# Row maxima turned by a product with the identity on TensorE, and their one transfer issued by ScalarE on its own queue

## The chip, the cores and the metric

The kernel runs on 1 core of one Trainium2 chip. The metric is the device time of one execution in microseconds (us). Engines are named as in the profile: PE is TensorE's matmul, PEld its weight load, DVE is VectorE, ACT is ScalarE, POOL is GpSimd, SP is SyncE, whose queue issues DMA transfers.

## The reference, cut to what matters

Two attentions over the same `x` (2048 tokens, 640 wide, 32 heads of 20) are mixed by a gate per token. A is causal attention inside segments of 512 tokens with a linear memory carried from segment to segment. B is sliding-window attention with a window of 256.

```python
x = A_x
g = sigmoid((x * gate_w).sum(-1, keepdims=True))
# A, per segment s of 512 tokens
p = softmax(qs @ ks.T * Dh**-0.5 + causal_mask)
o = gate * (phi(qs) @ M) / (phi(qs) @ z + 1e-6) + (1 - gate) * (p @ vs)
M, z = M + phi(ks).T @ vs, z + phi(ks).sum()
# B, window of 256
p = softmax(where(mask, q @ k.T * Dh**-0.5, -1e9));  o = p @ v
out = g * (a @ A_wo) + (1 - g) * (b @ B_wo)
```

Each softmax needs, for every query, the maximum of its row of scores before the exponent is taken. The change is about how these maxima reach the second score product.

## The kernel before, in words

**Stages and tiles.** The work is cut into 16 tiles `T`, four head groups (two of A, two of B) times four segments. For each tile, `gemm` (L429) projects q and k as three products of split float32 parts, `v_mm` (L543) projects v, and the parts of q and k are written to DRAM (`qk_store`, L477) and read back as stacks (`stack_read`, L604) with the head's dimension on partitions. Each tile then gives four units `u` of four heads, 64 units in all. A q stack `qst` has 123 used rows for each head: 120 hold the split parts of q, and the last three (from row `6 * DH`) hold the row maximum as three bfloat16 parts, so that the second score product subtracts the maximum by itself.

**A unit.** `max_mm` (L622) makes the scores once, queries on partitions, 16 products per unit. `max_red` (L633) on DVE adds the mask and takes the maximum over the keys, one column of the tile `mx` for each head and block of 128 queries: 16 columns on 128 partitions. These maxima have to be split into three bfloat16 parts and turned so that queries lie on the free axis, since they become rows of `qst`. Then `st_mm` (L687) makes the scores again with keys on partitions and the maxima subtracted, `st_exp` (L694) on ACT takes the exponent, `select` (L700, L703) on POOL clears what the mask forbids, `av_mm` (L717) multiplies by v, and `o_turn` (L796) to `o_store` (L836) divide and store. `o_load` (L849 to L860) reads the heads' outputs back for the output projection, again `gemm`, with results added by `y_out` (L868, L871).

**The maxima's way before the change.** `max_res` (L643, POOL) subtracts the upper bfloat16 half from the 16 maxima. `max_high` (L646, ACT) copies the upper halves of maximum and remainder into `mrs`, and `max_low` (L650, POOL) puts the third part there. `max_turn` (L654, DVE) transposes `mrs` in blocks of 32 by 32 into `mt`. `max_store` (L660, SP, two transfers) writes `mt` to DRAM as `dmx`, 64 bytes at a time, which finishes the turn. `max_rows` (L664, SP) waits until both have landed and reads three rows of `dmx` into `qst`. All transfers of the kernel are issued by SP, in one order.

**What sets the order.** `Plan` holds every step with a due time, the engine, an assumed duration and what it reads and writes. `Plan.order` (L94) walks through them like a list scheduler: of the steps whose inputs are there, the one that can start first comes next, and the earlier due time decides ties. Each engine gets its steps in that order, and runs them in that order on the chip whatever happens there. A transfer is modelled as landing a fixed time plus its share of 16 rings after its issue. So a step that is made shorter, or is moved to another engine, changes what the plan puts beside it, and the order of the whole program. Due times of the steps above are in units: the first products at `u - MT`, the maxima's way at `u - MS`, the second products from `u + 0.04`.

The two PE steps read and write PSUM banks, of which there are eight, dealt out by the plan by kind: `mx` three, `st` two, `misc` two, `pj` three to seven.

Of the kernel before, what the change touches and what calls it, by code (L numbers as in the profile page):

```python
# [20 lines left out]
DH = 20  # L21
S = 2048
L = 512
# [14 lines left out]
NPX, NMI, NOB = 7, 2, 2  # L38
# [16 lines left out]
class Plan:  # L55
# [13 lines left out]
    RINGS = 16  # L69

    def add(self, t, eng, dur, fn, *a, new=(), mod=(), put=(), get=(), size=0, pace=None, cols=0, ldw=(0.107, 0.2),
            bank=None, lazy=0.0, rings=16, packet=2048, port=False):
        if size:
            size = (size / packet / rings * (0.011 + packet / 21e3), rings)
        self.items.append((t, len(self.items), eng, dur, fn, a, new, mod, put, get, size, pace, cols, ldw, bank, lazy, port))

    TICK = 10.24 / 3
# [16 lines left out]
    def order(self):  # L94
# [85 lines left out]
        while len(out) < n:  # L180
            best = None
            for e, c in cand.items():
                cold = e == "pe" and self.cold(free[e])
                for i in c:
                    at = free[e]
                    if e == "pe":
                        at += max(0.0, items[i][13][0] - tail)
                    z = max(at, ready[i]) + (items[i][15] if tail > 0.06 else 0.0)
                    if items[i][16] and e in ("dve", "pool"):
                        z = max(z, port)  # L190
                    if items[i][14]:
                        k, most, _ = items[i][14]
                        if not avail or held.get(k, 0) >= most:
                            continue
                        z = max(z, min(avail.values()))
                    if e == "dve" and "|" in items[i][2]:
                        z += DP
                    z = (z, cold and items[i][12] < 900, i)
                    if best is None or z < best[0]:
                        best = (z, e)  # L200
            (start, _, i), e = best
            start -= DP if e == "dve" and "|" in items[i][2] else items[i][15] if e == "pe" and tail > 0.06 else 0.0
            if items[i][14]:
# [36 lines left out]
            if j is not None:  # L240
                ready[j] = max(ready[j], start)
                miss[j] -= 1
                if not miss[j]:
                    offer(j)
            for j in succ[i]:
                to = items[j][2]
                lag = ((0.0 if e == "pe" else XS) if to == e and not size else self.TO_PE if to == "pe" else
                       0.0 if size else self.FROM_PE if e == "pe" else self.OTHER)
                ready[j] = max(ready[j], done + lag)
                miss[j] -= 1  # L250
                if not miss[j]:
                    offer(j)
# [19 lines left out]
def attention(ctx, tc, const, dram, xt, wqk, wv, wo, beta, ident, o_dram, out):  # L272
# [17 lines left out]
            nc.tensor.matmul(p[:, 0:256], ones[:, 0:128], ones, start=True, stop=True)  # L290

    idf = const.tile([128, 128], F32, name="idf")

    mask_a = const.tile([128, 512], BF16, name="mask_a")
    mask_b = const.tile([128, 384], BF16, name="mask_b")
# [15 lines left out]
    def c_load():  # L311
        nc.sync.dma_start(idf, ident)
        nc.sync.dma_start(bet, bass.AP(tensor=beta.tensor, offset=beta.offset, ap=[[8, 4], [0, 32], [1, 8]]))

    def c_exp():
        nc.scalar.activation(gh[:, 0], bet, AF.Exp, scale=-1.0)

# [8 lines left out]
    vau = [stack.tile([128, n, VROW], F32, name=f"vau{i}") for i, n in enumerate((4, 6, 6))]  # L326


    mrs = [stack.tile([128, 64], BF16, name=f"mrs{i}") for i in range(2)]
# [8 lines left out]

    def init_m():
        nc.gpsimd.memset(pks, 0.0)  # L340
        for t in mrs:
            nc.gpsimd.memset(t, 0.0)

    def init_v(i):
        t = vau[i]
# [13 lines left out]
    NT = NSG * NSEG  # L359
    NU = 4 * NT  # L360
    PE, ACT, DVE, POOL, SP = "pe", "act", "dve", "pool", "sp"
    DI, DJ, SI = 0.48, 0.65, 0.53

    def unit(u):
        T, g = divmod(u, 4)
# [259 lines left out]
    def max_red(u, p, b, r):  # L625
        T, g, isb, s = unit(u)
        w = max_keys(u, b)[1]
        mk = mask_b[:, 384 - w:] if isb else mask_a[:, 512 - w:]
        if p == 0 and b == 0 and r == 0:
            B["M", u] = work.tile([128, 32], F32, name="mx", tag="mx")  # L630
        x = B["mx", u, p, b, r][:, :w]
        j = 4 * (2 * p + r) + b
        nc.vector.tensor_tensor_reduce(out=x, in0=x, in1=mk, scale=1.0,  # L633
                                       scalar=BIG, op0=ALU.add, op1=ALU.max, accum_out=B["M", u][:, j:j + 1])

    def high(x):

        return x.bitcast(BF16).rearrange("p (j c) -> p j c", c=2)[:, :, 1]

    def max_res(u):  # L640

        x = B["M", u]
        nc.gpsimd.tensor_tensor(out=x[:, 16:32], in0=x[:, 0:16], in1=high(x[:, 0:16]), op=ALU.subtract)  # L643

    def max_high(u):
        nc.scalar.activation(mrs[u % 2][:, 0:32], high(B["M", u]), AF.Copy)  # L646

    def max_low(u):
        x = B["M", u][:, 16:32]
        nc.gpsimd.tensor_tensor(out=mrs[u % 2][:, 32:48], in0=x, in1=high(x), op=ALU.subtract)  # L650

    def max_turn(u):
        t = B["mt", u] = work.tile([128, 64], BF16, name="mt", tag="mt")
        nc.vector.transpose(t, mrs[u % 2])  # L654

    def max_store(u, i):
        if i == 0:
            B["dmx", u] = dram.tile([4, 4, L], BF16, name="dmx", tag="dmx", bufs=3)
        d = B["dmx", u]
        nc.sync.dma_start(bass.AP(tensor=d.tensor, offset=d.offset + 8 * L * i, ap=[[32, 4], [128, 32], [1, 32]]),  # L660
                          B["mt", u][:, 32 * i:32 * i + 32])

    def max_rows(u):
        nc.sync.dma_start(qst[u % NQ][6 * DH:6 * DH + 3], B["dmx", u][0:3])  # L664

# [253 lines left out]
    add(-13, POOL, 2.0, c_mask, put=["mk"])  # L919
    add(-25, PE, 0.107 * WARM, c_warm, bank=("warm", 1, "warm"), cols=256 * WARM)  # L920
    add(-16.5, SP, 1.1, c_load, put=["cl"], size=2 ** 16)
    add(-3, ACT, 0.25, c_exp, get=["cl"], put=["ce"])
    add(-3, DVE, 1.2, c_fac, get=["cl", "ce"], put=["cf"])

# [62 lines left out]
    for u in range(NU):  # L987
# [12 lines left out]
                    new=[("M", 2, ("M", u))] if i == 0 and r == 0 else [],  # L1000
                    put=[("M", u)] if i or r else [])
        t = u - MS
        add(t, POOL, 0.2, max_res, u, mod=[("M", u)], port=True)
        add(t + .001, ACT, 0.24, max_high, u, get=[("M", u), "im"], new=[("mr", 2, ("mr", u))])
        add(t + .002, POOL, 0.2, max_low, u, get=[("M", u)], put=[("mr", u)], port=True)
        add(t + .01, DVE, 0.165, max_turn, u, get=[("mr", u)], new=[("mt", 2, ("mt", u))])
        for i in range(2):
            add(t + .03 + .001 * i, SP, DJ, max_store, u, i, get=[("mt", u)], size=8192, packet=64,
                new=[] if i else [("dmx", 3, ("dmx", u))], put=[("dmx", u)] if i else [])
        add(t + .04, SP, DJ, max_rows, u, get=[("dmx", u)], put=[("qr", u)], size=12288, packet=1024, rings=3)  # L1010
        for i in range(6):
            b, p = divmod(i, 2)
            t = u + 0.04 + i / 6
# [103 lines left out]
```

## Time and profile before

| | |
|---|---|
| time, median of 3 runs | 1183.43 us (1181.92 to 1185.99) |
| the profiled execution | 1172.0 us, span 1170.3 us |
| mean granted TensorE clock | 0.982 |
| busy: PE, POOL, DVE, ACT | 1095.5, 815.5, 780.8, 703.7 us |
| DMA | 221.35 MB, all but the code on one queue, 74.5% of 16 engines' span |

Busy time of an engine leaves out its waits and the issuing of transfers. A wait is put down to what ended last before the waiting instruction could start. In the view of waits each row has who waited, for whom, us in total, how often, and the longest. In the chain of waits each row has the start in us from the span's begin, the length, and what the program's end depended on then. In the view by windows each row has the stretch, busy time of each engine, the granted clock, the DMA engines' share and GB/s. In the groups each row ends with busy us, mean ns of one, and the idle time of the engine before them.

### The profile page before, as it was taken

To read this page: it belongs to the slowest core of one execution; us is meant where nothing else is said; L and a number is where in the kernel's file an instruction comes from. 1 tells how busy PE (TensorE), PEld (TensorE's weight loads), DVE (VectorE), ACT (ScalarE), POOL (GpSimd) and SP (SyncE) were. 2 spreads that over 40 slices of the span, in tenths; PEclk is the share of its full clock that TensorE was granted. 3 is DMA by queue.
4 is the path that set the end of the run, shared out by engine and by line. 5 is a ranking of instruction groups with operands and counts; after the bars stand their busy time and mean duration, and the time that the engine had idled before them with its cause. 6 is when DMAs were issued, how large, how long until landed. Compare 5 with 4: busy or idle time off the path is not lost.

```text
span 1170.3 us, 25017 instructions
## 1 busy us (share of the span) xinstructions
PE 1095.5 (94%) x8322; PEld 717.0 (61%) x8322; DVE 780.8 (67%) x2641; ACT 703.7 (60%) x1495; POOL 815.5 (70%) x1063
## 2 busy tenths in 40 slices
PE   9788999997999999999898999998997999999996
PEld 7564666664655666556565566655664666766664
DVE  3475877765778667786586866777664776577711
ACT  6246575675557765575664767665664595655651
POOL 9345484796667786678774778667795686866874
PEclk9999999998999999999899999999998999999999
DMA  6877588878988589877788867888577885887523
GB/s 211 163 188 182 162 207 198 202 185 160 240 203 208 149 217 233 217 196 207 147 217 176 234 163 186 206 223 204 148 176 203 219 215 140 205 205 211 161 91 108
DMA packets 228081, 221.35 MB, mean 189 GB/s; under 512 B 80240, under 2 KB 189168, under 8 KB 227952
## 3 DMA queue, kind: packets, MB, share of 16 engines
q1 hardware_dynamic: 227952, 219.75, 74.5%
q8 instruction: 66, 1.08, 0.4%
q14 instruction: 63, 0.52, 0.2%
HBM read 154.73 MB, written 64.95 MB: 188 GB/s over the span
## 4 chain that ended last, share of the span: by engine, by line
PE 58%; DMA 23%; POOL 6%; DVE 5%; SPq 4%; issue 3%; ACT 2%; POOLq 0%; ACTq 0%; DVEq 0%
PE bank L429 22%; PE bank L687 10%; PE bank L717 9%; PE bank L622 8%; PE bank L543 8%; DMA qst<-dmx 3%; DMA qst<-dqk 3%; DMA dmx<-mt 3%; DMA xst<-wv 3%; DVE bank L633 3%; DMA kst<-dqk 2%; DMA wst<-wqk 2%; DMA xst<-o_dram 2%; DMA xst<-xt 1%; SPq L604 1%
## 5 line engine op out<-in xcount | busy, mean ns | idle before, releaser
L694 ACT ACTIVATE P<-bank 128x512 f32<-128x512 f32 (+2 forms) x768 | 372.0, 563 | 94.1 <-PE bank L687 80.0
L429 PE MATMUL bank<-xhl,w 128*128 128x512 f32 x1200 | 366.4, 431 | 1.8 <-POOL xhl L394 0.6
L633 DVE CUSTOM_DVE_ANT_0 bank<-bank,mask_b 128x384 f32<-128x384 f32 (+2 forms) x512 | 259.3, 552 | 53.0 <-PE bank L622 51.9
L633 DVE CUSTOM_DVE_ANT_0 bank<-bank,mask_a 128x128 f32<-128x128 f32 (+3 forms) x512 | 237.9, 511 | 71.6 <-PE bank L622 70.3
L622 PE MATMUL bank<-kst,qst 120*128 120x384 bf16 (+3 forms) x1024 | 253.1, 312 | 21.1 <-DVE mx L633 9.8
L687 PE MATMUL bank<-qst,kst 123*128 123x384 bf16 (+2 forms) x1216 | 233.0, 291 | 36.7 <-DMA qst<-dmx 28.3
L429 PEld LDWEIGHTS bank<-xhl,w 128*128 128x128 f32 x1200 | 219.2, 193 | 46.5 <-issue 1.7
L394 POOL TENSOR_TENSOR w<-wst,w 128x640 fp32r<-128x640 f32 x119 | 185.3, 1558 | 70.2 <-ACT w L378 63.0
L700 POOL TENSOR_SCALAR_AFFINE_SELECT P<-P 128x512 f32<-128x512 f32 x256 | 160.7, 636 | 79.5 <-ACT P L694 76.3
L543 PE MATMUL bank<-wv,xhl 128*128 128x320 f32 (+1 forms) x960 | 189.5, 335 | 1.3 <-POOL wv L394 0.7
L429 PE MATMUL bank<-ohl,w 128*128 128x512 f32 x600 | 178.9, 425 | 5.9 <-POOL w L394 2.6
L687 PEld LDWEIGHTS <-kst 123*128 123x128 bf16 x1216 | 92.0, 99 | 138.4 <-issue 74.0
L717 PE MATMUL bank<-P,vau 128*32 128x384 f32 (+3 forms) x2432 | 160.8, 408 | 1.8 <-POOL P L703 0.9
L543 PEld LDWEIGHTS bank<-wv,xhl 128*128 128x128 f32 x960 | 152.5, 192 | 12.3 <-DVE mx L633 2.7
L622 PEld LDWEIGHTS <-qst 120*128 120x128 bf16 x1024 | 81.5, 98 | 123.8 <-issue 86.6
L633 DVE DVE_READ_ACCUMULATOR2_ANT mx<- 128x1 f32 x1024 | 142.8, 140 | 0.0
L446 POOL TENSOR_TENSOR hl<-res,hl 128x512 bf16<-128x512 f32 x104 | 121.2, 1167 | 30.3 <-ACT hl L378 28.0
L796 DVE STREAM_TRANSPOSE ot<-bank 128x512 f32<-128x512 f32 x88 | 62.7, 714 | 99.3 <-PE bank L717 94.6
L429 PEld LDWEIGHTS bank<-ohl,w 128*128 128x128 f32 x600 | 108.8, 191 | 31.4 <-POOL ohl L394 5.0
L378 ACT ACTIVATE w<-wst 128x640 fp32r<-128x640 f32 x121 | 89.9, 744 | 54.5 <-PE bank L429 17.7
L717 PEld LDWEIGHTS bank<-P,vau 128*32 128x32 f32 x2432 | 68.8, 110 | 83.8 <-issue 66.3
L394 POOL TENSOR_TENSOR wv<-xst,wv 128x322 fp32r<-128x322 f32 x79 | 68.3, 877 | 34.6 <-ACT wv L378 32.5
(73 smaller groups left out, 910.8 us busy)
## 6 DMA issues: line engine op xcount, KB each, us to landing
wst<-wqk SPq DMA_DIRECT2D x80, 320.0 KB
o_dram<-ot SPq DMA_DIRECT2D x64, 256.0 KB
qst<-dqk SPq DMA_DIRECT2D x64, 240.0 KB
kst<-dqk SPq DMA_DIRECT2D x64, 240.0 KB
wst<-wo SPq DMA_DIRECT2D x41, 320.0 KB
xst<-wv SPq DMA_DIRECT2D x80, 161.0 KB
dqk<-hl SPq DMA_DIRECT2D x32, 384.0 KB
qst<-dqk SPq DMA_DIRECT2D x64, 160.0 KB
```

The lines of the kernel that those rows point to most:

```text
L378: nc.scalar.activation(dst, src, AF.Copy)
L394: EN[e].tensor_tensor(out=t[:, 1], in0=B.pop(src), in1=f(t[:, 0]), op=ALU.subtract)
L429: nc.tensor.matmul(p, w[:, a, col:col + 128], x[:, b], start=(c == 0 and i == 0), stop=(c == NC - 1 and i == 2))
L446: EN[e].tensor_tensor(out=t[:, 2], in0=B["res", k], in1=t[:, 1], op=ALU.subtract)
L543: nc.tensor.matmul(p[:, :n], x[:, a, 128 * b:128 * b + 128], w[:, bb, :n], start=(c == 0 and i == 0), stop=(c == NC - 1 and i == 2))
L622: nc.tensor.matmul(pt[:, :n], qst[u % NQ][0:6 * DH, h, 128 * b:128 * b + 128], kst[u % NK][0:6 * DH, h, c0:c0 + n], start=True, stop=True)
L633: nc.vector.tensor_tensor_reduce(out=x, in0=x, in1=mk, scale=1.0, scalar=BIG, op0=ALU.add, op1=ALU.max, accum_out=B["M", u][:, j:j + 1])
L687: nc.tensor.matmul(pt[:, c:c + 128 * n], kst[u % NK][0:6 * DH + 3, h, c0:c0 + 128], q[0:6 * DH + 3, h, 128 * q0:128 * (q0 + n)], start=Tru ...
L694: nc.scalar.activation(B["P", u, b][:, 2 * p + r, c0:c1], B["st", u, b, p, r][:, c0:c1], AF.Exp, scale=SCALE)
L700: nc.gpsimd.affine_select(out=v, in_=v, pattern=[[0, 4], [1, 128]], compare_op=ALU.is_ge, fill=0.0, base=0, channel_multiplier=-1)
L717: nc.tensor.matmul(o[32 * j:32 * j + 32, 128 * q0:128 * (q0 + n)], v[:, VA * h:VA * h + 32], t[:, j, c:c + 128 * n], start=(b == 0 and i = ...
L796: nc.vector.transpose(B["ot", u][:, i].rearrange("p b e -> p (b e)"), B["o" if i == 0 else "num", u])
```

## The change

The upper halves of the maxima need no copy: they are read in place by `high`, a view of every second bfloat16 in `mx`. So `mx` gets 48 columns, and two subtractions on POOL, one after the other, leave maximum, first remainder and second remainder there. `max_turn` is now a product on PE: the 48 upper halves are its weights, a bfloat16 identity of 128 by 128 (`idb`, made once by ACT from `idf`) streams through, and 48 rows of 128 queries come out in a PSUM bank of the kind `misc`. `max_out` on ACT copies them to `mt` in SBUF. `max_rows` is one transfer of 48 rows of 256 bytes from `mt` straight to the three rows of `qst`, issued by ACT. `mrs`, `dmx`, the two stores to DRAM, the copy and the transpose are gone. In the plan, a transfer marked `side` doesn't queue on the 16 modelled rings: it lands 1.2 us and twice its own time after its issue, and the usual fixed part later.

```diff
-            size = (size / packet / rings * (0.011 + packet / 21e3), rings)
+            size = (size / packet / rings * (0.011 + packet / 21e3), rings, side)
...
-                took, rings = size
-                done = 0.0
-                for k in range(rings):
+                took, rings, side = size
+                done = start + dur + 1.2 + 2 * took if side else 0.0
+                for k in range(0 if side else rings):
...
-    def max_res(u):
+    def max_res(u, i):
         x = B["M", u]
-        nc.gpsimd.tensor_tensor(out=x[:, 16:32], in0=x[:, 0:16], in1=high(x[:, 0:16]), op=ALU.subtract)
+        a = x[:, 16 * i:16 * i + 16]
+        nc.gpsimd.tensor_tensor(out=x[:, 16 * i + 16:16 * i + 32], in0=a, in1=high(a), op=ALU.subtract)
-    def max_high(u):
-        nc.scalar.activation(mrs[u % 2][:, 0:32], high(B["M", u]), AF.Copy)
-    def max_low(u):
-        x = B["M", u][:, 16:32]
-        nc.gpsimd.tensor_tensor(out=mrs[u % 2][:, 32:48], in0=x, in1=high(x), op=ALU.subtract)
     def max_turn(u):
-        t = B["mt", u] = work.tile([128, 64], BF16, name="mt", tag="mt")
-        nc.vector.transpose(t, mrs[u % 2])
-    def max_store(u, i):
...
+        nc.tensor.matmul(psum(("mp", u))[0:48, 0:128], high(B["M", u]), idb, start=True, stop=True)
+    def max_out(u, e):
+        t = B["mt", u] = work.tile([48, 128], BF16, name="mt", tag="mt")
+        copy(e, t, B["mp", u][0:48, 0:128])
     def max_rows(u):
-        nc.sync.dma_start(qst[u % NQ][6 * DH:6 * DH + 3], B["dmx", u][0:3])
+        nc.scalar.dma_start(qst[u % NQ][6 * DH:6 * DH + 3].rearrange("p h (b t) -> p (h b) t", b=4), B["mt", u])
...
-        add(t, POOL, 0.2, max_res, u, mod=[("M", u)], port=True)
-        add(t + .001, ACT, 0.24, max_high, u, get=[("M", u), "im"], new=[("mr", 2, ("mr", u))])
-        add(t + .002, POOL, 0.2, max_low, u, get=[("M", u)], put=[("mr", u)], port=True)
-        add(t + .01, DVE, 0.165, max_turn, u, get=[("mr", u)], new=[("mt", 2, ("mt", u))])
         for i in range(2):
-            add(t + .03 + .001 * i, SP, DJ, max_store, u, i, get=[("mt", u)], size=8192, packet=64,
-                new=[] if i else [("dmx", 3, ("dmx", u))], put=[("dmx", u)] if i else [])
-        add(t + .04, SP, DJ, max_rows, u, get=[("dmx", u)], put=[("qr", u)], size=12288, packet=1024, rings=3)
+            add(t + .001 * i, POOL, 0.2, max_res, u, i, mod=[("M", u)], port=True)
+        add(t + .01, PE, 0.06, max_turn, u, bank=("misc", NMI, ("mp", u)), get=[("M", u), "id"], cols=102, ldw=(0.02, 0.05))
+        add(t + .02, ACT, 0.22, max_out, u, "act", get=[("mp", u)], new=[("mt", 2, ("mt", u))])
+        add(t + .03, ACT, DQ, max_rows, u, get=[("mt", u)], put=[("qr", u)], size=12288, packet=256, rings=3, side=True)
```

The order moves everywhere. Three places at the last unit, 63, show how. On PE before the change, ahead of the first second score product of unit 63 (L687 with `qst3` and `kst3`) stand output projections (L429) and unit 62's product with v (L717, tile `vau2`):

```order
L429 MATMUL bank_15422<-ohl_15312,w_15135 128x512 x3
L429 MATMUL bank_15422<-ohl_15318,w_15135 128x512 x3
L717 MATMUL bank_15455<-P_15370,vau2_97 32x384 x4
L717 MATMUL bank_15455<-P_15370,vau2_97 32x128 x4
L717 MATMUL bank_15455<-P_15396,vau2_97 32x384 x4
L717 MATMUL bank_15455<-P_15396,vau2_97 32x128 x4
L717 MATMUL bank_15455<-P_15426,vau2_97 32x256 x8
L687 LDWEIGHTS kst3_90
L687 MATMUL bank_15489<-qst3_94,kst3_90 128x384
```

On PE in the change, the turn of unit 63's maxima (L650) stands in the same row of work, and the second score products (now L680) follow after one projection (now L431, three products) and unit 62's product with v (now L710, 24 instructions, which are 48 products in the trace):

```order
L431 MATMUL bank_15277<-ohl_15211,w_15101 128x512 x3
L650 LDWEIGHTS mx_15068
L650 MATMUL bank_15308<-idb_83,mx_15068 48x128
L431 MATMUL bank_15277<-ohl_15259,w_15101 128x512 x3
L710 MATMUL bank_15330<-P_15218,vau2_98 32x384 x4
L710 MATMUL bank_15330<-P_15218,vau2_98 32x128 x4
L710 MATMUL bank_15330<-P_15253,vau2_98 32x384 x4
L710 MATMUL bank_15330<-P_15253,vau2_98 32x128 x4
L710 MATMUL bank_15330<-P_15286,vau2_98 32x256 x8
L680 LDWEIGHTS kst3_91
L680 MATMUL bank_15357<-qst3_95,kst3_91 128x384
```

So PE itself now has a step of the maxima's way, in the middle of its other work, and what it does between the turn and the scores is given by this row. On SP before the change, unit 63's two stores (L660) and its read (L664) stand among loads of heads' outputs (L857, L860) and a store of them (L836):

```order
L660 DMA dmx_15355<-mt_15353 4x32x32
L860 DMA xst_15358<-o_dram1_63 120x1x512
L857 DMA xst_15358<-o_dram1_63 8x512
L857 DMA xst_15372<-o_dram1_63 12x512
L860 DMA xst_15372<-o_dram1_63 100x1x512
L857 DMA xst_15372<-o_dram1_63 16x512
L660 DMA dmx_15355<-mt_15353 4x32x32
L857 DMA xst_15401<-o_dram1_63 4x512
L860 DMA xst_15401<-o_dram1_63 120x1x512
L857 DMA xst_15401<-o_dram1_63 4x512
L836 DMA o_dram1_63<-ot_15364 128x512
L664 DMA qst3_94<-dmx_15355 3x2048
```

On SP in the change (L853, L850 and L829 are the lines that were L860, L857 and L836; L867 stores results, L388 loads weights) nothing of the maxima is left:

```order
L853 DMA xst_15238<-o_dram1_63 100x1x512
L850 DMA xst_15238<-o_dram1_63 16x512
L867 DMA out<-ys_14390 128x512
L388 DMA wst_15262<-wo 128x640
L829 DMA o_dram1_63<-ot_15220 128x512
L850 DMA xst_15315<-o_dram1_63 4x512
L853 DMA xst_15315<-o_dram1_63 120x1x512
L850 DMA xst_15315<-o_dram1_63 4x512
```

The transfer stands on ACT instead, behind the exponents of unit 62 (L687 now, tile `P`) and right behind the copy of the turned maxima (L380, tile `mt`):

```order
L687 ACTIVATE P_15286<-bank_15274 128x512
L687 ACTIVATE P_15286<-bank_15288 128x512
L687 ACTIVATE P_15286<-bank_15294 128x512
L380 ACTIVATE mt_15311<-bank_15308 48x128
L657 DMA qst3_95<-mt_15311 3x16x128
L861 ACTIVATE ys_15324<-bank_15277 128x512
L380 ACTIVATE w_15326<-wst_15140 128x640
```

What moved there: the way from turned maxima to `qst` left DVE and SP, and now leads over PE and ACT, each of which has other steps of its order ahead of it. At other units up to eight other steps of ACT stand between the copy and the transfer; at 53 of the 64 it is one or none.

More of the change, by code (lines that the diff above doesn't have):

```diff
@@ L71, in add @@
     def add(self, t, eng, dur, fn, *a, new=(), mod=(), put=(), get=(), size=0, pace=None, cols=0, ldw=(0.107, 0.2),
-            bank=None, lazy=0.0, rings=16, packet=2048, port=False):
+            bank=None, lazy=0.0, rings=16, packet=2048, port=False, side=False):
         if size:
-            size = (size / packet / rings * (0.011 + packet / 21e3), rings)
+            size = (size / packet / rings * (0.011 + packet / 21e3), rings, side)
         self.items.append((t, len(self.items), eng, dur, fn, a, new, mod, put, get, size, pace, cols, ldw, bank, lazy, port))
@@ L292, in attention @@
     idf = const.tile([128, 128], F32, name="idf")
+    idb = const.tile([128, 128], BF16, name="idb")
     mask_a = const.tile([128, 512], BF16, name="mask_a")
@@ L313, in c_load, with c_id @@
         nc.sync.dma_start(bet, bass.AP(tensor=beta.tensor, offset=beta.offset, ap=[[8, 4], [0, 32], [1, 8]]))
+    def c_id():
+        nc.scalar.activation(idb, idf, AF.Copy)
     def c_exp():
@@ L326, in attention @@
     vau = [stack.tile([128, n, VROW], F32, name=f"vau{i}") for i, n in enumerate((4, 6, 6))]
-    mrs = [stack.tile([128, 64], BF16, name=f"mrs{i}") for i in range(2)]
     pks = stack.tile([128, L], F32, name="pks")
@@ L340, in init_m @@
         nc.gpsimd.memset(pks, 0.0)
-        for t in mrs:
-            nc.gpsimd.memset(t, 0.0)
     def init_v(i):
@@ L361, in attention @@
     PE, ACT, DVE, POOL, SP = "pe", "act", "dve", "pool", "sp"
-    DI, DJ, SI = 0.48, 0.65, 0.53
+    DI, DJ, SI, DQ = 0.48, 0.65, 0.53, 0.4
     def unit(u):
@@ L629, in max_red @@
         if p == 0 and b == 0 and r == 0:
-            B["M", u] = work.tile([128, 32], F32, name="mx", tag="mx")
+            B["M", u] = work.tile([128, 48], F32, name="mx", tag="mx")
         x = B["mx", u, p, b, r][:, :w]
@@ L921, in attention @@
     add(-16.5, SP, 1.1, c_load, put=["cl"], size=2 ** 16)
+    add(-3, ACT, 0.25, c_id, get=["cl"], put=["id"])
     add(-3, ACT, 0.25, c_exp, get=["cl"], put=["ce"])
```

5 lines of the change are left out of this document (removed).

## The prediction

> **What bounds the kernel now.** First the page's busy times, then who made PE wait, then the stretches in which it waited.
>
> ```profile
> span 1170.3 us, 25017 instructions
> PE 1095.5 (94%) x8322; PEld 717.0 (61%) x8322; DVE 780.8 (67%) x2641; ACT 703.7 (60%) x1495; POOL 815.5 (70%) x1063
> PE bank L687 <- DMA qst<-dmx: 28.3, 10, 7.7
> PE bank L622 <- DVE mx L633: 9.8, 10, 7.5
> PE bank L687 <- DVE mx L633: 4.9, 5, 2.7
> PE bank L622 <- DMA kst<-dqk: 3.9, 2, 2.9
> PE bank L687 <- ACT P L694: 2.0, 4, 0.8
> ```
>
> PE is busy for 1095.5 of 1170.3 us, so 74.8 us of idle time are all that a change of waits can win, but for the clock. The largest single part, 28.3 us in 10 waits, is the second score product waiting for the read of the maxima from DRAM, the very transfer that the change replaces. The next, DVE's maxima, make 14.7 us in two rows. Where do they lie?
>
> ```profile
> 260.00:345.00 85.00, 75.64 (x565) 48.62 (x563) 56.03 (x194) 46.13 (x108) 55.16 (x73) 0.94 0.84 198
> 560.00:600.00 40.00, 34.77 (x281) 23.21 (x280) 22.09 (x73) 24.91 (x55) 26.35 (x39) 0.91 0.80 167
> 860.00:900.00 40.00, 32.29 (x230) 21.41 (x220) 18.57 (x66) 20.80 (x45) 24.75 (x33) 0.91 0.85 197
> 1127.00:1171.00 44.00, 34.01 (x171) 23.44 (x169) 5.12 (x8) 11.11 (x19) 21.31 (x19) 0.99 0.31 93
> ```
>
> In the first three stretches PE is idle for 9.4, 5.2 and 7.7 us, and its granted clock is 0.94, 0.91 and 0.91: the waits also bring half clock. Put as time at half clock, 0.09 missing in 40 us is 7.2 us, twice, and 0.06 in 85 us is 10.2 us, together 24.6. The chain of waits shows what happens there, and at the last unit and two others:
>
> ```profile
> 571.45 8.80 DMA qst<-dmx
> 872.64 9.42 DMA dmx<-mt
> 882.13 7.37 DMA qst<-dmx
> 1059.58 2.44 DMA qst<-dmx
> 1114.12 4.04 DMA dmx<-mt
> 1118.23 2.83 DMA qst<-dmx
> ```
>
> Each unit's maxima go through two transfers, one after the other: 16.8 us in the middle of the kernel, 6.9 at its end, where the fourth stretch shows the DMA engines at 0.31. A 12 KB read takes 2.44 to 2.83 us with little ahead of it, and 7.37 to 8.80 in the queue that everything shares.
>
> **The change part by part.** The sum is made against the profiled execution, 1172.0 us, which is 11.4 below the median of the three runs shown; I carry the difference over to that median.
>
> *The waits for `qst<-dmx`.* They go with the transfer: -28.3. What is late next at those places is counted below as new waits.
>
> *Half clock.* Of the 24.6 us, part was idle anyway, and the rest did half the work. At most 12 us come back, at least nothing; I take -4, since the waits themselves fill most of those windows.
>
> *The tail.* Unit 63's way from first store to scores is 6.9 us at 1114, and becomes shorter by 2 to 3 us for each transfer saved. Behind it PE is idle for 10.0 of the last 44 us, but other work fills part of what is won: -4, between 0 and -6.5.
>
> *64 products on PE.* The nearest rows are products of the chain, weight loads included:
>
> ```profile
> 595.22 0.45 PE bank L687 x4
> 603.37 0.43 PE bank L622 x2
> 591.90 1.40 PE bank L429 x6
> 586.82 1.33 PE bank L543 x9
> 601.08 2.29 PE bank L717 x32
> 588.85 2.73 PE bank L717 x48
> 598.91 0.39 PE bank L755 x32
> L622 PEld LDWEIGHTS <-qst x1024: 95/98/152, 41.7 to 1105.8; 120*128 120x128 bf16 x171
> ```
>
> A product of 48 weights and 128 columns lies between 0.39/32 = 0.012 us (32 columns) and 0.45/4 = 0.113 (256 on average). It is nearest to the latter: 0.1, so 64 x 0.1 = +6.4, between 0.8 and 13.8 (0.43/2 each, at the upper end).
>
> *A new wait on PE, for POOL.* `max_turn` stands in PE's order behind both subtractions, and behind it wait all products that follow. What waited for them until now:
>
> ```profile
> DVE mt L654 <- POOL mrs L650: 37.8, 19, 6.9
> ACT mrs L646 <- POOL mx L643: 29.3, 21, 4.3
> PEld bank L717 <- POOL P L700: 3.4, 8, 0.9
> PEld bank L717 <- POOL P L703: 2.8, 5, 1.0
> ```
>
> DVE lost 37.8 us so. PE as the fullest engine tends to come late: for POOL's selects, which stand in front of 64 groups of products with v, its loads wait 6.2 us in 13 waits, 0.5 us each. Between 0 and 37.8, nearer to PE's own rows: +8.
>
> *A new wait on PE, for the new transfer.* This decides most. The plan now leaves less PE work between turn and scores. At unit 63 it is one projection and one product with v: 1.40/2 + 2.73 = 3.4 us. Counting the order's steps the same way by the rows above for all 64 units (an estimate; the memory's small products left out) gives 3.4 to 10.9 us, a quarter below 5.1, the median 5.9. If the way from turn to landing takes 4 us in each unit, the shortfalls add up to 2.2 us; with 5 us to 11.9, with 6 to 37.8, with 7 to 73.9. The way is: the copy, the exponent that mostly stands behind it, the issue, the landing, and what ACT still has to do when the turn is done.
>
> ```profile
> L646 ACT ACTIVATE mrs<-mx 128x32 bf16<-128x32 bf16 x64 | 15.0, 234 | 29.5 <-POOL mx L643 29.3
> L694 ACT ACTIVATE P<-bank 128x512 f32<-128x512 f32 (+2 forms) x768 | 372.0, 563 | 94.1 <-PE bank L687 80.0 <-PE bank L717 12.1
> L660 SPq DMA_DIRECT2D dmx<-mt x128: 506/528/3692, 61.5 to 1114.1; - x128
> L664 SPq DMA_DIRECT2D qst<-dmx x64: 232/270/1204, 80.1 to 1118.2; - x64
> L654 DVE STREAM_TRANSPOSE mt<-mrs 128x64 bf16<-128x64 bf16 x64 | 15.1, 235 | 38.5 <-POOL mrs L650 37.8 <-ACT mrs L646 0.5
> ```
>
> That is 0.23 + 0.56 + 2.44 to 2.83, since the quoted landings hold their issue, so 3.2 to 3.6; ACT's backlog, up to two exponents, makes it 3.2 to 4.8, if ACT's queue has nothing ahead of the transfer. Towards the upper end I take +6. If the landing is as late as in SP's queue, it is the second rival.
>
> *ACT.* A copy of 0.23 us goes and a similar one comes. The issue is new: 64 times 0.27 to 0.53, 17 to 34 us, on an engine that is busy for 703.7 of 1170.3. ACT's idle time hides it; without that cover exponents come later, and PE, which now loses 2.0 us to them, would pay.
>
> *DVE, POOL, SP.* DVE loses 64 transposes, 15.1 us, and its wait; it waits mostly for PE, so nothing. POOL's two subtractions stay; a bfloat16 copy of the identity at the start, two cleared tiles less and a `misc` bank more per unit cost nothing that I can find a row for, since that bank is freed by one copy. SP loses 128 x 0.528 + 64 x 0.270 = 84.9 us of issue, and its stop for the stores' landing, so loads start earlier; of PE's waits on loads (3.9 us for `kst`) some may go. I take nothing.
>
> *Sum.* -28.3 - 4 - 4 + 6.4 + 8 + 6 = -15.9: 1156.1 on the scale of the profiled execution, and 1183.43 - 15.9 = 1167.5 on that of the median.
>
> On queues, the Trainium skill has a rule that speaks against this. Its page "DMA: Bandwidth & Descriptors", section "Issuing engines are not separate DMA queues", says that starting transfers on several engines only saves the time of the issue, since all run on the same 16 DMA engines. By it alone the landing stays late, and the sum would be the second rival's. The same page, section "Queues, rings and completion order", says that each DMA engine takes turns between queues, packet by packet; by that the new transfer passes SP's backlog, and the sum is 1167.5. The rows before have one queue only, so no run here shows which holds.
>
> **The rivals.**
>
> *PE waits for POOL (slower).* PE reaches the turn before POOL's second subtraction, as DVE did 19 times. In favour: the plan places it where it thinks the input just ready, and POOL is busy for 70% of the span. Against: the 0.5 us of PE's present waits for POOL. With 37.8 in place of 8 the sum is +13.9: 1197. It decides from about 24 us on, 0.37 us per unit. Chance 0.09.
>
> *The transfer lands no earlier on ACT's queue (slower).* With the DMA engines at 0.80 to 0.85, as in the stretches above, and landings like the 7.37 and 8.80 us above, the way takes 6 us or more. Then 37.8 replaces 6 in the sum: +15.9, so 1199. It decides from about 5.4 us, where the shortfalls reach the 21.9 us that are left. This is the rule's case. In favour: the load. Against: the late landings above stood behind SP's own transfers. Chance 0.13.
>
> *The next transfer is late instead (no change).* At the same places the next stacks or loads hold PE up, as the 3.9 us for `kst` show they can; the DMA engines have nearly the same bytes to move, 1 MB less (128 stores of 128 x 32 x 2 bytes). All of the 28.3 us and the clock come back as other waits, and the other terms are small: 1183. Against: SP gets 84.9 us of its issue time back. Chance 0.10.
>
> **How the numbers follow.** The forecast has 0.68. A measurement of this kernel can tell 0.3% from no change, 3.6 us. Faster: 0.68 and 0.01 of the third rival, 0.69; the same: 0.08 of it; slower: 0.09 + 0.13 + 0.01 = 0.23. The likeliest time is 1167.5. Its own range is 1149 to 1183: favourable terms (clock -8, tail -6, PE +4, new waits 2 each) give -34; the unfavourable (clock and tail 0, +8, +12, +8) give 0. Reaching 8 in 10 needs part of the slower cases: 1149 to 1190.
>
> **What would show it.** The waits of L680 on `qst<-mt` say whether the landing is early: below 10 us in all I am right, above 25 wrong. PE's wait for POOL's `mx` at L650 should be near 8 us. The granted clock in the middle should rise to 0.99 and above. If PE's idle time doesn't fall below 65 us, the sum is wrong.

## The result, and the profile after

The changed kernel takes 1228.33 us (median of 6 runs, 1226.11 to 1240.88), the kernel before 1182.82 (6 runs on the same chip, 1181.92 to 1185.99): a ratio of 1.040, 95% interval 1.035 to 1.044. It is slower by some 45 us where I forecast a gain of 16. The profiled execution took 1230.83 us.

First the page's span and PE's busy time, and the two queues that now carry data; SP's is q1, ACT's q10, the columns behind the name being packets, MB and share:

```profile
span 1229.1 us, 24887 instructions
PE 1120.6 (91%) x8386; PEld 735.0 (60%) x8386; DVE 774.8 (63%) x2581; ACT 714.9 (58%) x1492; POOL 816.2 (66%) x1061
q1 hardware_dynamic: 210672, 217.91, 70.0%
q10 hardware_dynamic: 3264, 0.79, 0.3%
```

PE's idle time is 1229.1 - 1120.6 = 108.5 us, 33.7 more than before, and PE is busy for 25.1 us more. The waits of PE in the changed kernel say what the idle time is for:

```profile
PE bank L680 <- DMA qst<-mt: 23.9, 16, 3.6
PE bank L624 <- DMA kst<-dqk: 21.1, 11, 6.9
PE bank L650 <- POOL mx L646: 13.0, 3, 11.6
PE bank L624 <- ACT P L687: 12.3, 8, 6.4
PE bank L680 <- ACT P L687: 7.2, 6, 3.1
PE bank L624 <- DVE mx L635: 3.3, 8, 1.5
PE bank L680 <- DVE mx L635: 0.8, 3, 0.3
```

The 28.3 us for `qst<-dmx` went, and 23.9 us for the new transfer came. That alone would be a small gain. But the wait for the k stacks rose from 3.9 to 21.1 us, that for ACT's exponents from 2.0 to 12.3 + 7.2, and 13.0 us for POOL's maxima are new, 11.6 of them once, at the start. Only DVE's maxima got better, 14.7 to 4.1. The stretches in the middle, where PE was at full clock before, lost it. The view by windows of the changed kernel, and then the same stretch of the kernel before (us, busy of PE, PEld, DVE, ACT, POOL, granted clock, DMA share, GB/s):

```profile
600.00:860.00 260.00, 232.18 (x1819) 151.64 (x1817) 169.37 (x556) 150.68 (x314) 170.12 (x216) 0.95 0.74 184
900.00:1050.00 150.00, 138.77 (x967) 90.09 (x965) 95.92 (x319) 88.62 (x187) 100.44 (x132) 0.97 0.70 179
```

```profile
600.00:860.00 260.00, 245.56 (x1952) 161.04 (x1954) 184.84 (x603) 161.08 (x337) 189.32 (x240) 1.00 0.76 192
```

No engine is busier in that stretch than it was. All of them do less, the DMA engines too: something that feeds them all stands still. All transfers but the new one come from SP, so the next view is what SP's queue waited for in the changed kernel:

```profile
SPq L606 <- DMA qst<-mt: 73.8, 16, 6.8
SPq L388 <- DMA qst<-mt: 33.3, 10, 6.3
SPq L719 <- DMA qst<-mt: 19.0, 5, 5.0
SPq L829 <- DMA qst<-mt: 18.5, 5, 6.6
SPq L727 <- DMA qst<-mt: 13.2, 3, 6.3
SPq L504 <- DMA qst<-mt: 7.4, 2, 5.2
```

With three smaller rows (2.9, 2.7, 2.3) these are 173.1 us; the expectations below name 158, the five largest. L388 loads weights, L829 stores a head's output, L606 reads other units' stacks: none of them needs the maxima that ACT's transfer carries, and SP waits for its landing all the same. The program's order with its waits shows by what. These are one transfer of ACT, the one of SP behind it and the one eight places later (no view of the profile, so in a plain fence; the numbers are places in the program's order of all transfers of SP and ACT):

```
848 ACT L657 DMA qst3_95<-mt 3x16x128 [counts on DMAHW7; waits Activation]
849 SP  L727 DMA qfs<-dphq [counts on DMAHW0; waits DMAHW0]
...
856 SP  L388 DMA wst<-wqk 128x640 [counts on DMAHW7; waits Pool, DMAHW7]
```

This program has eight counters for the transfers of SP and ACT, DMAHW0 to DMAHW7, and these take them in turn in this order, whichever of the two issues them. A transfer that takes a counter again waits until the one before on that counter has landed. So when ACT's transfer has its turn, the transfer eight places later, one of SP in 63 cases of 64, can't be issued before ACT has come to it and it has landed. ACT comes to it behind POOL's subtractions, PE's turn and its own exponents. SP is a single queue in a fixed order, and everything behind that place waits too.

In the trace ACT issued transfer 848 at 813.21 us, and SP, done with issuing transfer 855 at 814.85 us, issued 856, the load of weights, at 818.12 us. The trace's records bear it out for all: SP's 1133 and ACT's 64 transfers name the same eight semaphores, and in every wait of the rows above SP waited for the semaphore on which its own waiting transfer counts.

### The profile page after: what moved, and what is told of

It is laid out like the page before. It is cut to its first block, busy times and chain, and to the rows that moved or that the text cites. A ratio compares the mean times of both kernels' runs of the same rounds, so it can differ in the third digit from the quotient of the medians.

```text
span 1229.1 us, 24887 instructions
## 1 busy us (share of the span) xinstructions
PE 1120.6 (91%) x8386; PEld 735.0 (60%) x8386; DVE 774.8 (63%) x2581; ACT 714.9 (58%) x1492; POOL 816.2 (66%) x1061
## 4 chain that ended last, share of the span: by engine, by line
PE 52%; DMA 28%; POOL 6%; ACT 4%; SPq 4%; DVE 3%; issue 3%; ACTq 0%; POOLq 0%; DVEq 0%
PE bank L431 21%; DMA qst<-mt 8%; PE bank L680 8%; PE bank L624 8%; PE bank L545 7%; PE bank L710 7%; DMA kst<-dqk 5%; DMA xst<-wv 2%; DMA wst<-wqk 2%; SPq L606 2%; ACT P L687 2%; DMA dqk<-hl 2%; DMA xst<-o_dram 2%; DMA qst<-dqk 2%; DVE bank L635 1%
## 5 line engine op out<-in xcount | busy, mean ns | idle before, releaser
L687 ACT ACTIVATE P<-bank 128x512 f32<-128x512 f32 (+2 forms) x768 | 381.6, 550 | 170.5 <-PE bank L680 116.5
L431 PE MATMUL bank<-xhl,w 128*128 128x512 f32 x1200 | 366.3, 433 | 1.1 <-ACT xhl L380 0.5
L624 PE MATMUL bank<-kst,qst 120*128 120x384 bf16 (+3 forms) x1024 | 263.2, 318 | 44.1 <-DMA kst<-dqk 21.1
L680 PE MATMUL bank<-qst,kst 123*128 123x384 bf16 (+2 forms) x1216 | 237.0, 293 | 34.9 <-DMA qst<-mt 23.9
L431 PEld LDWEIGHTS bank<-xhl,w 128*128 128x128 f32 x1200 | 222.2, 194 | 46.0 <-issue 2.0
L545 PE MATMUL bank<-wv,xhl 128*128 128x320 f32 (+1 forms) x960 | 196.4, 340 | 0.6 <-DVE mx L635 0.2
L431 PE MATMUL bank<-ohl,w 128*128 128x512 f32 x600 | 180.4, 429 | 5.7 <-POOL ohl L396 3.0
L680 PEld LDWEIGHTS <-kst 123*128 123x128 bf16 x1216 | 92.7, 99 | 146.6 <-issue 91.8
L545 PEld LDWEIGHTS bank<-wv,xhl 128*128 128x128 f32 x960 | 155.5, 195 | 14.1 <-DVE mx L635 2.3
L710 PE MATMUL bank<-P,vau 128*32 128x384 f32 (+3 forms) x2432 | 159.9, 407 | 0.0
L448 POOL TENSOR_TENSOR hl<-res,hl 128x512 bf16<-128x512 f32 x104 | 121.2, 1167 | 28.8 <-ACT hl L380 28.3
L431 PEld LDWEIGHTS bank<-ohl,w 128*128 128x128 f32 x600 | 111.5, 193 | 32.2 <-POOL ohl L396 4.9
L380 ACT ACTIVATE w<-wst 128x640 fp32r<-128x640 f32 x121 | 89.2, 738 | 58.4 <-DMA wst<-wqk 29.6
L710 PEld LDWEIGHTS bank<-P,vau 128*32 128x32 f32 x2432 | 68.8, 110 | 79.5 <-issue 65.5
```

Source lines behind the costliest of these rows:

```text
L380: nc.scalar.activation(dst, src, AF.Copy)
L431: nc.tensor.matmul(p, w[:, a, col:col + 128], x[:, b], start=(c == 0 and i == 0), stop=(c == NC - 1 and i == 2))
L448: EN[e].tensor_tensor(out=t[:, 2], in0=B["res", k], in1=t[:, 1], op=ALU.subtract)
L545: nc.tensor.matmul(p[:, :n], x[:, a, 128 * b:128 * b + 128], w[:, bb, :n], start=(c == 0 and i == 0), stop=(c == NC - 1 and i == 2))
L624: nc.tensor.matmul(pt[:, :n], qst[u % NQ][0:6 * DH, h, 128 * b:128 * b + 128], kst[u % NK][0:6 * DH, h, c0:c0 + n], start=True, stop=True)
L680: nc.tensor.matmul(pt[:, c:c + 128 * n], kst[u % NK][0:6 * DH + 3, h, c0:c0 + 128], q[0:6 * DH + 3, h, 128 * q0:128 * (q0 + n)], start=Tru ...
```

## The experiments

Theory A is this hold by the shared counters. Theory B is the second rival in a wider form: the transfer lands too late for the PE work that the plan puts between turn and scores. Theory C is ACT's time for the issue, which the view of the tile `mt` gives as much more than I had put in:

```profile
L380 ACT ACTIVATE mt<-bank x64: 255/271/289, 64.2 to 1176.7; 48x128 bf16<-48x128 f32 x64
L657 ACTq DMA_DIRECT2D qst<-mt x64: 728/729/1343, 64.5 to 1177.0; - x64
```

All ratios are to the kernel before, run on the same chip.

| kernel | median us | ratio, 95% interval |
|---|---|---|
| the change | 1228.33 | 1.040 (1.035 to 1.044) |
| e1: GpSimd issues, order as in the change | 1252.56 | 1.064 (1.060 to 1.068) |
| e2: SP issues, order as in the change | 1258.97 | 1.070 (1.064 to 1.075) |
| e4: before + an extra transfer by ACT | 1241.52 | 1.053 (1.048 to 1.059) |
| e5: before + the same by GpSimd | 1188.09 | 1.008 (1.004 to 1.012) |
| e12: before + the same by SP | 1189.92 | 1.006 (1.003 to 1.009) |
| e8: before + 64 copies on ACT | 1187.51 | 1.003 (1.001 to 1.006) |
| e7: ACT issues, landing planned 4 us later | 1221.46 | 1.033 (1.029 to 1.038) |
| e9: e7's order, GpSimd issues | 1191.00 | 1.007 (1.004 to 1.009) |
| e6: a step of GpSimd, planned 4 us later | 1177.49 | 0.995 (0.992 to 0.998) |
| e3: a step of SP | 1187.52 | 1.004 (1.000 to 1.007) |
| e10: as e6, 6 us later | 1186.82 | 1.001 (0.999 to 1.004) |
| e11: as e6, maxima due earlier | 1197.77 | 1.012 (1.007 to 1.017) |

**e1 and e2: another issuer, nothing else moved.** In both, one word of the changed kernel is replaced:

```diff
     def max_rows(u):
-        nc.scalar.dma_start(qst[u % NQ]...
+        nc.gpsimd.dma_start(qst[u % NQ]...        # e1; nc.sync in e2
```

> The changed kernel with every engine's order kept; only the issuer of the one transfer is GpSimd instead of ACT. Theory A (the eight completion counters are shared by all of SP's and ACT's transfers in turn, so SP's queue stands until ACT's transfer has landed): GpSimd's transfers count on other counters, SP's waits on the stacks' transfer go from 158 us to under 20, and the time falls from 1228 to 1165 to 1190. Theory B (the transfer simply lands too late for the scores, whoever issues it): 1215 to 1245, PE's waits on it stay at 24 us or grow. Theory C (ACT's issue of 0.73 us each, 47 us in all, holds up ACT's exponents): 1195 to 1215, ACT's share of PE's waits falls by 20 us while SP's waits stay.

> The changed kernel with every engine's other instructions kept in their order; SP issues the one transfer, at the place where it stood in the written order. Theory A: SP now waits for ACT's copy at that place instead of for the landing eight places later; the wait is shorter by the landing (about 2 us for 64 transfers) and by ACT's issue, so 1190 to 1215, with SP's waits on the copy of 60 to 120 us in the place of the 158 us. Theory B: 1220 to 1245, since the landing comes no earlier on SP's queue. Theory C: 1200 to 1215, since ACT is rid of the issue.

Both came out slower than the change, and so above what any of the theories gave: 1252.56 and 1258.97. SP has no wait on the transfer in e1, and GpSimd's 64 transfers name eight semaphores of their own; that part of A came true, the time did not. The waits of PE in e1 have the reason in their first row, and the last row of its tile `mt` has the landing:

```profile
PE bank L680 <- DMA qst<-mt: 55.5, 28, 5.9
```

```profile
DMA to landing us min/median/max: 2.2/4.7/9.5
```

PE waits 55.5 us on the transfer in place of 23.9. Pairing the records of the turn and of the issue in order of time gives the way up to the issue: the median is 1.5 us from the turn's start with GpSimd, 0.7 with ACT, 1.3 with SP (there 4.5 in one case of ten, since SP has its other transfers ahead). With the landing, e1's way is about 6.2 us, the sum of both medians, and the order has 4.8 us of PE work there at the median by the plan's durations, 5.9 by the prediction's count from rows of the trace before. So the landing is too late here as B has it, and A alone falls: taking SP's hold away gains nothing in this order, while PE's wait on the transfer grows by 31.6 us. In e2, PE's row has 73.1 us. There SP also stood for 53.5 us at L657 waiting for ACT, since it meets the transfer in its own fixed order: e2 swaps one hold of SP for another, and says little about the counters.

**e4, e5, e8, e12: the hold by itself, in the kernel before.** The way of the maxima stays as it was. A transfer of 48 rows of 256 bytes whose result nobody reads is added per unit, issued by ACT (e4), GpSimd (e5) or SP (e12); e8 has a copy on ACT in its place:

```diff
     def max_high(u):
         nc.scalar.activation(mrs[u % 2][:, 0:32], high(B["M", u]), AF.Copy)
+        nc.scalar.dma_start(ddst, dsrc)           # e4; nc.gpsimd in e5, nc.sync in e12
+        nc.scalar.activation(dsrc, dsrc, AF.Copy) # e8 alone, dsrc 128 x 384
```

> The kernel before, with one further transfer in every unit that nobody uses: 48 rows of 256 B from SBUF to SBUF, issued by ACT right behind its copy of the maxima's upper halves. Theory A: SP's transfer eight places later waits until ACT has come to it and it has landed, so SP's waits on that transfer are 60 to 150 us in all and the time goes from 1183 to 1195 to 1220. Theory B: no one waits for the transfer, so within 4 us of 1183. Theory C: ACT's 64 issues of 0.73 us cost up to 47 us of ACT; 1183 to 1195, without waits of SP on the transfer.

> The control to the extra transfer of ACT: the same transfer, at the same place in the written order, issued by GpSimd. Theory A: GpSimd's transfers count on counters of their own, so SP waits for none of them and the time is 1180 to 1192. Theory B: the same, 1180 to 1188. Theory C: 1180 to 1190, since ACT issues nothing.

> The second control to ACT's extra transfer: in its place ACT has 64 further copies of some 0.5 us, as long as the issue was (0.51 us), and no transfer. Theory A (the counters): within 8 us of the kernel before. Theory C (ACT's time for the issue): as far up as the extra transfer of ACT, 1225 to 1245.

> The third control to ACT's extra transfer: the same transfer at the same place in the written order, issued by SP itself. It takes a counter of the same eight, but SP issues it in its own turn, so no other engine's lateness can reach SP's queue; its source is ready at once. Theory A (a counter shared with a later engine): SP pays 64 issues of some 0.5 us (33 us), most of it in its free time, and 1183 to 1197. If any further transfer on these eight counters costs what ACT's did (a shorter reach of the eight): 1215 to 1245.

The same bytes, at the same place in the written order, cost 5.3% from ACT, 0.8% from GpSimd and 0.6% from SP, and 64 copies on ACT, which made it busy for 26 us more where e4's issues took 64 x 0.51 = 33, cost 0.3%. A gave too little for e4 (1195 to 1220, measured 1241.52), and its other three ranges held; C, which gave e8 1225 or more, is out as the main cause. What SP's queue waited for in e4:

```profile
SPq L607 <- DMA ddst<-dsrc: 45.9, 12, 6.0
SPq L389 <- DMA ddst<-dsrc: 33.7, 11, 5.0
SPq L840 <- DMA ddst<-dsrc: 18.5, 4, 7.1
SPq L738 <- DMA ddst<-dsrc: 15.5, 6, 4.7
```

With seven smaller rows it is 147.6 us of waits for a transfer that nobody needs. In e5 there is no such row, and in e12 a single wait of 1.4 us. ACT itself was not held: in all 64 units the issue began before ACT's instruction ahead of it had ended. So what PE pays in e4 comes by way of SP: its wait for the old transfer, which SP issues, is 55.5 us against 27.0 in e5, 28.5 of the 35.5 us by which PE is idle longer.

```profile
PE bank L691 <- DMA qst<-dmx: 55.5, 18, 8.8
```

```profile
PE bank L691 <- DMA qst<-dmx: 27.0, 11, 7.7
```

**e7 and e9: more PE work before the scores, with and without the hold.** e7 changes one number of the plan in the changed kernel. e9 is e7 with GpSimd as the issuer in the same place of the same order.

```diff
-                done = start + dur + 1.2 + 2 * took if side else 0.0
+                done = start + dur + 5.2 + 2 * took if side else 0.0
```

> The changed kernel, ACT the issuer, with one number of the plan changed: the landing is reckoned 4 us later, and the plan sets 8.1 us of PE's work (median) between the turn and the scores. Theory A: SP's waits on the transfer stay (120 to 180 us), and the time stays at 1210 to 1235. Theory B: PE's waits on the transfer go, and the time falls to 1165 to 1190.

> The kernel in which the plan reckons the landing 4 us later (1221 with ACT as the issuer), every engine's order kept, and only the issuer of the one transfer changed to GpSimd, in the place where ACT's issue stood in the written order. Theory A (the shared counters cost the 44 us that are left between 1221 and 1177): SP's waits on the transfer go from some 170 us to under 20 and the time to 1170 to 1195. If the 44 us come from the order that the planner made for ACT: 1210 to 1230.

With A and B as rivals, e7 speaks for A: PE no longer waits for the transfer, and the time is still 1221.46. Its waits of PE, of ACT and of SP's queue, two rows each:

```profile
PE bank L680 <- ACT P L687: 25.2, 9, 7.0
PE bank L680 <- DMA qst<-mt: 0.4, 1, 0.4
ACT wv L380 <- DMA xst<-wv: 57.7, 15, 15.5
ACT w L380 <- DMA wst<-wqk: 32.2, 10, 6.3
SPq L606 <- DMA qst<-mt: 94.2, 18, 7.7
SPq L388 <- DMA qst<-mt: 43.6, 12, 10.2
```

SP waits for the transfer for 208.0 us in nine rows. And the same rows of e9, where SP has none:

```profile
PE bank L680 <- ACT P L687: 13.1, 5, 6.9
PE bank L680 <- DMA qst<-mt: 4.7, 5, 1.7
ACT wv L380 <- DMA xst<-wv: 47.8, 16, 16.2
ACT w L380 <- DMA wst<-wqk: 19.3, 8, 5.6
```

One word is the difference, and it is worth 1.033 against 1.007, some 30 us. It also takes 47 us of issues off ACT; e8's 26 us of copies there had cost 0.3%. The rows fit this way: SP issues loads late, ACT waits for `wst` and `xst` (12.9 and 9.9 us more), the exponents that stand behind those steps in ACT's order are late, and PE, which lost 0.4 us to the transfer, loses 12.1 us more to ACT. The chains of waits agree. e7's goes through the transfer for 6.3% of 1223.6 us, though PE waits for it only once, and e9's for 2.1% of 1194.3:

```profile
by line: PE bank L431 21.3%; PE bank L624 8.2%; PE bank L680 8.2%; PE bank L710 7.8%; PE bank L545 7.8%; DMA qst<-mt 6.3%; DMA kst<-dqk 4.0%; DMA qst<-dqk 3.9%; issue 3.0%; DMA xst<-o_dram 2.1%; DMA wst<-wqk 2.1%; DVE bank L635 2.0%; ACT P 
...
595.71 10.18 DMA qst<-mt
```

```profile
by line: PE bank L431 23.1%; PE bank L680 9.0%; PE bank L710 8.9%; PE bank L624 8.5%; PE bank L545 7.8%; DMA kst<-dqk 6.1%; DMA qst<-dqk 5.8%; DVE bank L635 3.5%; DMA xst<-wv 3.2%; issue 2.4%; DMA qst<-mt 2.1%; DMA dqk<-hl 1.8%; SPq L606 1.
```

With the change and e1 these are two choices of issuer with two plans: ACT 1.040 and 1.033, GpSimd 1.064 and 1.007. With the hold in place the later landing in the plan wins 0.6%, without it 5.7%. So hold and late landing are both real, and each hides what the other costs.

**e3, e6, e10, e11: both causes taken away.** In e6 the planner places the transfer on GpSimd and reckons its landing 4 us later. e10 has 6 us, e11 has e6 with `MT, MS = 1.5, 0.78`. In e3 it is a step of SP, with SP's usual reckoning.

```diff
-        add(t + .03, ACT, DQ, max_rows, u, ..., packet=256, rings=3, side=True)
+        add(t + .03, POOL, DI, max_rows, u, ..., packet=256, rings=3, side=True)  # e6, with 5.2 for 1.2
+        add(t + .03, SP, DJ, max_rows, u, ..., packet=256, rings=3)               # e3
```

> The transfer is a step of GpSimd, placed by the planner, which is told that it lands 4 us later than it reckoned. Both causes are gone if there are two: SP shares no counter with it, and the plan sets 7.7 us of PE's work (median) between the turn and the scores in place of 4.8. Theory A and theory B together: 1150 to 1180, PE's waits on the transfer under 15 us. Theory A alone, with the landing no matter: the same as with GpSimd as the issuer in the written order, 1252. If the product, ACT's copy or POOL's second step cost the time instead: 1215 or more.

> The changed kernel with the one transfer written as a step of SP, which the planner places by its costs for SP's queue, with the landing at the rings' end as it reckons for all of SP's transfers; the orders of all engines follow anew. Theory A (an issuer beside SP whose transfers count on SP's eight counters holds SP): no such hold is left, and the plan sets SP's place for it; 1160 to 1190. Theory B (what counts is the PE work that the plan sets between the turn and the scores): the plan here sets 6.1 us (median) in place of 4.8, less than what a turn to a landing takes, so 1195 to 1225.

> GpSimd as the issuer, placed by the planner, with the landing reckoned 6 us later in place of 4. PE waited 3.7 us on the transfer at 4, so there is nothing to win there, and the scores come later in the order: 1175 to 1195. If the transfer's longest landings (11.9 us) still cost at 4: 1165 to 1177.

> GpSimd as the issuer with the landing reckoned 4 us later, and maxima and turn due 0.2 of a unit earlier (about 3.6 us): the plan sets 8.5 us of PE's work (median) between turn and scores in place of 7.7. The stacks are needed earlier by the same, and PE waited 8.5 us for kst: 1172 to 1195, a gain only if the waits on ACT's exponents (15.8 us) come from the scores being late.

e6 takes 1177.49 us, 0.5% below the kernel before and, by the two ratios, 4.3% below the change: both causes together are the loss, and product, copy and POOL's second step, which e6 keeps, are not. It is the best version found. e3 is within A's range, and B's number for it fell: PE waited 1.8 us for the transfer there, since the planner reckons SP's landing unit by unit. e10 gains nothing; in e6 only 3.7 us of PE's waits were left for the transfer. e11 missed its range on the slow side; what earlier maxima cost there wasn't followed up. Why e6 gains no more, its page and its waits of PE show:

```profile
span 1175.6 us, 24993 instructions
...
PE 1104.8 (94%) x8386; PEld 726.3 (62%) x8386; DVE 786.1 (67%) x2598; ACT 706.7 (60%) x1495; POOL 835.6 (71%) x1105
```

```profile
PE bank L680 <- ACT P L687: 15.8, 5, 7.1
PE bank L650 <- POOL mx L646: 11.9, 4, 9.9
PE bank L624 <- DMA kst<-dqk: 8.5, 3, 5.8
PE bank L624 <- ACT P L687: 3.7, 4, 1.4
PE bank L680 <- DMA qst<-mt: 3.7, 3, 2.4
```

PE's idle time is 70.8 us against 74.8. The 28.3 us of the old wait are down to 3.7 for the new one, and came back as waits for exponents, for POOL's maxima at the start, and for stacks; PE itself is busy for 9.3 us more. That is the third rival, "the next transfer is late instead", with other work in the transfer's part.

## Why the prediction was wrong

**The step that failed** is the paragraph on DVE, POOL and SP: "SP loses ... 84.9 us of issue, and its stop for the stores' landing, so loads start earlier ... I take nothing." SP did lose those issues. But a transfer on another engine's queue didn't leave SP's queue alone, as the sum took for granted: SP waited 173.1 us for it, since both queues' transfers take the same eight counters in turn. The term that I put at nothing, with a hope of less, measured 30 us by e9 against e7 (1.007 and 1.033), and 53 us in the kernel before by e4 against e5 (1241.52 and 1188.09, on the same chip). The wait was to be found beforehand, in SP's queue of the kernel before:

```profile
SPq L386 <- DMA kst<-dqk: 13.3, 18, 1.7
SPq L477 <- DMA kst<-dqk: 12.8, 16, 2.9
```

L386 loads weights there, which need no k stack, and L477 stores parts of q and k. So the counters held SP already, for 1.7 and 2.9 us at most as long as every transfer was SP's own; ACT's held it for up to 6.8. I asked where each moved step was queued, and not what else its transfer shares with the queue it left.

**The new wait on PE, for the new transfer** (+6) measured 23.9 us in the changed kernel, near the 25 that I had set as wrong. The way was longer than 3.2 to 4.8 us. From the turn's start to the issue it took 0.7 us at the median and 2.4 in one case of ten. From the issue to the end of the last of its 51 packets, by the records of q10, it took 3.2 us at the median, 4.1 at three quarters, 5.6 at nine tenths and 8.2 at the longest, and the landing was reported 0.6 us later at the median. Turn to landing makes 5.1 us at the median and 7.2 at nine tenths. I had taken 2.44 to 2.83 for issue and landing from two reads with little ahead of them. The shortfall table fits: 6 us gave 37.8, 5 gave 11.9. So this term was mis-sized too, and its price shows only without the hold: with ACT as the issuer e7 took the wait away and won 0.6% of the time of before (1.040 to 1.033, with intervals that overlap), with GpSimd the same step of the plan won 5.7% (e1 to e9).

**The landing and the two queues.** The Trainium skill's section "Issuing engines are not separate DMA queues" (page "DMA: Bandwidth & Descriptors") says that the transfers of all issuing engines run on the same 16 DMA engines and interleave. I had drawn a late landing from it, and the landing was later than I reckoned, 3.2 us at the median to the last packet. The Trainium skill's section "Queues, rings and completion order", same page, has the queues served in turn, packet by packet. That fits those figures too: the packets were through in 3.2 us while q1 took 70% of the DMA engines' time. Neither bears on the hold.

**The other terms.** *The waits for `qst<-dmx`*: gone, as put (-28.3). *64 products on PE*: 0.1 us each was too little. PE's group is 0.24 us each, and the next product starts 0.17 us after the turn's start at the median of all 64, 11 us where I put 6.4:

```profile
L650 PE MATMUL bank<-idb,mx x64: 237/238/303, 63.9 to 1176.0; 128*48 128x128 bf16 x64
```

```profile
908.17 0.17 PE bank L650
908.34 0.65 PE bank L545 x3
```

*PE's wait for POOL* (+8): 13.0, but 11.6 of it in one wait at the start; the rest is 1.4, so PE doesn't come to the turn as early as DVE did, and the first rival is out. *Half clock* (-4): the wrong sign, 0.95 in the middle where it was 1.00, in the stretches with the new idle times. That lengthens the products too: PE is busy for 25.1 us more, of which the turns are 11, and in e4, which has no turns, for 28.4 us more at a granted clock of 0.953 against 0.982. *ACT*: the issue took 0.73 us each, 47 us and not 17 to 34. Its cover held: e8 put as many copies of 0.4 us there (ACT's busy time 730.1 against 703.7 us) and lost 0.3%. *The tail* (-4) can't be told apart in a kernel in which everything is late.

**The rivals.** The second one, with 0.13, named the right side and a real wait; its 1199 was 29 us short, and it had no part for SP. The hold by the counters was in none of them.

**What stays open.** How the loss in the changed kernel divides between hold and plan has no single answer: with the order as it was, taking the hold away made it slower (e1), and with the hold in place a better order won 0.6% (e7). ACT's transfers take the same counters, and could have held ACT; they did not: in the changed kernel and in e7 every one of the 64 was issued within 0.03 us of the end of ACT's instruction ahead of it, most of them before that end. What ACT's 47 us of issues cost in the changed kernel wasn't measured apart, since they leave ACT together with the hold; e8 put 26 us there, in the kernel before. Why e1 and e2 are slower than the change itself is read from PE's wait rows alone.

## What to carry to other kernels

Before a transfer is moved to another engine's queue, look in the program's waits for what ties it to the queue that it leaves: where completion counters are shared in turn, a transfer that depends on a late engine holds the queue of the engine that was never late. Adding the transfer alone, with nobody reading it, to the kernel before tells hold, bytes and issue apart. Where two causes cover for each other, take both away at once, since each alone can look like the wrong one (1.064 and 1.033, together 1.007, and 0.995 with GpSimd's place planned).

## What the runs showed of the hardware

The issue of the same small transfer differs by engine and form. 48 rows of 256 bytes from SBUF into three rows of SBUF took 0.73 us on ACT, 0.63 on GpSimd and 0.78 on SP, and with 48 rows as the target 0.51 on ACT, 0.56 on GpSimd and 0.59 on SP; the read of 12 KB from DRAM had taken 0.27 on SP. In e5 GpSimd's issues took 64 x 0.56 = 36 us of an engine that was busy for 72% of the span with them, and the kernel lost only 0.8%. From GpSimd's issue to the landing the transfer took 2.2 us at the least, 4.7 to 5.4 at the median and 9.5 to 12.0 at the most in e1, e6 and e9.
